# Attention and cosine FFN: conversions, splits and first gates tied to later products, mask added in PSUM

## The chip, the cores and the metric

The kernel runs on one core of one Trainium2 chip. The metric is the device time of one execution in microseconds (us); lower is better. Engines are named as in the profile: PE is TensorE (PEld its weight loads), DVE is VectorE, ACT is ScalarE, POOL is GpSimd, SP issues the DMA transfers.

## The reference

```python
scores = q @ k.T / sqrt(64)                       # 8 batches, 8 heads, 576 tokens, 64 per head
scores = where(mask[h], scores, -1e9)             # heads 0-3: the last 32 positions; heads 4-7: every 32nd position
attn = exp(scores - max) / (sum + 1e-9)
x = (attn @ v).transpose(0, 2, 1, 3).reshape(4608, 512)
h = x @ w_in                                      # 512 x 2048
out = (h * cos(h)) @ w_out                        # 2048 x 512
```

The weights arrive as 8-byte numbers (float64) and are turned into float32 on the chip. Every large product is made of fp32r values split into a high and a low part, as hi·hi + hi·lo + lo·hi.

## The kernel before

**Two phases.** Phase 1 (0 to about 521 us of the profiled execution) computes attention and h = x·w_in, and stores h to DRAM (`h_all`). Phase 2 (to 916 us) reads h back in 512-token pieces, computes g = h·cos(h) (`gate`), splits it, and multiplies by w_out (`outer`, line 583).

**Phase 1 by slots.** After a prologue that computes the attention of batch 0, a loop runs over slots, 56 per batch: 8 blocks `f` of 256 columns of h by `STEP` = 7 products. A product is 6 matmuls of 128x288 into a bank of PSUM (`m` three buffers, `n` and `o` one each). Batch 0 uses plain products (`FirstBlock`, line 470), the others a Winograd form with 7 products per block (`Block`, line 499): the products n0, n1 ... n6 stand at `SLOTS`, and after each `after0` ... `after6` copy a bank to SBUF on ACT (`kept`, line 507: m1, n1, m2) or finish a half of h (`hidden`: DVE line 517, ACT line 515). So n1's copy must end before the bank `n` is written by n4, three slots later, and the sum h<-m,n1 on DVE must end before n1's one SBUF tile is written by the next block.

**Other work between the slots.** Attention of the next batch comes as bursts of small matmuls some 8 slots apart (5 in batch 0), with a softmax on DVE, ACT and POOL (lines 236 to 256). In batches 0 and 1 the mask is written to PSUM by a matmul (line 226); from batch 2 on DVE adds it while it copies the scores to SBUF (line 244), takes the maximum (line 245), and POOL subtracts it (line 246). At the end of each batch the seven operands of the next (`x_hi`, `x_lo`) are formed (`Operands.sum` on DVE, line 431, and `make`, a split: ACT line 148, POOL line 149). In batch 0 each piece of w_in is loaded and converted (`to_float32`: two ACT steps, lines 133 and 139, two DVE steps, lines 140 and 143), split, and summed for the Winograd form (`weight_sums`); in batches 2 to 7 the same conversion goes over w_out, one piece per 17 slots, and the result is stored to DRAM (`w_all`), to be read and split in batch 7 (`output_weights`), in groups of three. The first three gates are issued in the last 14 slots of batch 7.

**Order.** A scheduler orders each engine's instructions by its own estimate of times. `order(later, first, ...)` adds a dependency without a semaphore that holds an instruction behind another in that schedule; `in_turn` chains all matmuls of the main loop, and `turn` is the last one. Only the first ACT step of a conversion is tied so (line 138).

Of the kernel before, what the change touches and what calls it, by code (L numbers as in the profile page):

```python
# [13 lines left out]
F32 = mybir.dt.float32  # L14
# [12 lines left out]
P = 128  # L27
# [36 lines left out]

UNITS = 7
# [13 lines left out]
def attention_cos_ffn(ctx, tc, qkl, vl, qkvs, w_in, w_out, eye, eye16, mask_l0, mask_l, mask_s, out):  # L79
# [45 lines left out]
    def to_float32(cv, src, out, bits=None):  # L125
        raw = cv.tile([P, 512, 2], I32, name="raw", bufs=3)
        load = nc.sync.dma_start(out=raw.rearrange("p n w -> p (n w)"), in_=src)
        if len(loads) == UNITS:
            order(load, loads[-1], "units first")
        low, top = raw[:, :, 0], raw[:, :, 1]  # L130
        scaled = top.bitcast(F32)
        bits = low if bits is None else bits
        begun = nc.scalar.activation(
            out=bits, in_=low.bitcast(U32), func=AF.Copy, scale=2.0 ** -29 * (1.0 - 2.0 ** -16),
            bias=7.5 * 2.0 ** -16 - 0.5,
        )
        if turn is not None:
            order(begun, turn, "with this product")
# [14 lines left out]
    def input_weights(cv, f, i):  # L153

        if i == 0:
            both = wp.tile([P, 6, 2 * P], I32, name="v")[:, :4]
            w = wp.tile([P, 2, 4, 2 * P], F32R, name="w")
            whole.append(both)
            wi.append(w)
        both, w = whole[f], wi[f]  # L160
        part = slice(2 * i, 2 * i + 2)
        name = "no"[i if f > 1 else 0]
        to_float32(
            cv, w_in.bitcast(I32)[2 * f + i], both[:, part].rearrange("p k n -> p (k n)"),
            pools[name].tile([P, 512], I32, name=name),
        )
        split(both[:, part].bitcast(F32), w[:, 0, part], w[:, 1, part])
        if i == 1:
            whole[f] = [both[:, n].bitcast(F32) for n in range(4)]
            wi[f] = [(w[:, 0, n], w[:, 1, n]) for n in range(4)]  # L170

    def weight_sums(cv, f, part):

        a11, a12, a21, a22 = whole[f][:4]
        if part == 0:
            sums = cv.tile([P, 3, 2 * P], F32, name="sums")
            whole[f].append(sums)
            s2, s3 = (sums[:, n] for n in range(2))
            first = nc.gpsimd.tensor_tensor(out=s3, in0=a11, in1=a21, op=ALU.subtract)
            order(first, turn, "with this product")  # L180
            nc.gpsimd.tensor_tensor(out=a21, in0=a21, in1=a22, op=ALU.add)
            split(a21, *wi[f][2])
            nc.gpsimd.tensor_tensor(out=s2, in0=a22, in1=s3, op=ALU.subtract)
        else:
            sums = whole[f][4]
            first = nc.gpsimd.tensor_tensor(out=sums[:, 2], in0=a12, in1=sums[:, 0], op=ALU.subtract)
            order(first, turn, "with this product")
            w = wp.tile([P, 2, 3, 2 * P], F32R, name="v")
            split(sums, w[:, 0], w[:, 1])
            wi[f] += [(w[:, 0, n], w[:, 1, n]) for n in range(3)]  # L190
# [5 lines left out]
    class Attention:  # L196
# [25 lines left out]
        def score_bank(self, b, mask):  # L222
            if b < 2:
                bank = self.bank(self.scores)
                n, w = mask.shape[1:]
                self.pe(nc.tensor.matmul(
                    bank[:, :n * w].rearrange("p (t w) -> p t w", w=w), ident16, mask, start=True, stop=False,
                    skip_group_check=True,
                ))
                return bank  # L230
            if self.kept is None:
                self.kept = self.bank(self.scores)
                nc.vector.memset(self.kept, 0.0)
            return self.kept

        def softmax(self, b, s, mask, n, w, pn=None):
# [33 lines left out]
        def local(self, b, u):  # L270
# [9 lines left out]
            def score(t, c):  # L280
                p, j = divmod(c, 2)
                self.scored = self.pe(nc.tensor.matmul(  # L282
                    s_ps[quarter_of(c), t * KW:(t + 1) * KW], q_t[half(j), p, QB * t:QB * (t + 1)],
                    k_t[half(j), p, QB * t:QB * t + KW], start=b > 1, stop=True, skip_group_check=True,
                ))
# [36 lines left out]
        def strided(self, b, p, u):  # L322
# [10 lines left out]
            def score(t, i):  # L333
                self.scored = self.pe(nc.tensor.matmul(  # L334
                    s_ps[half(1 - i, GB), t * GB:(t + 1) * GB], q_t[half(i), t], k_t[half(i), t],
                    start=b > 1, stop=True, skip_group_check=True,
                ))
# [73 lines left out]
    class Operands:  # L411
# [28 lines left out]
        def prepare(self, n):  # L440
            if n in (1, 3, 5, 6):
                self.sum(n)
            self.make(n)

# [38 lines left out]
    class Block:  # L483
# [21 lines left out]
        def kept(self, name):  # L505
            t = ev.tile([P, TH], F32, name=name)
# [38 lines left out]
    def whole_output_weights(cv, n):  # L545
        t = cv.tile([P, 3, 2 * P], F32, name="sums")[:, :2].rearrange("p k n -> p (k n)")
        to_float32(cv, w_out.bitcast(I32)[n], t.bitcast(I32))
        nc.sync.dma_start(out=w_all[n], in_=t)

    def output_weights(landed, g):  # L550
        w = wp.tile([P, 2, 4, 2 * P], F32R, name="w").rearrange("p f (l m) n -> p f l (m n)", l=2)
        v = wp.tile([P, 2, 3, 2 * P], F32R, name="v").rearrange("p l m n -> p (l m n)")
        parts = [v[:, :2 * DM].rearrange("p (l n) -> p l n", l=2), w[:, 0], w[:, 1]]
        for n in range(min(WG, NFC - WG * g)):
            both = landed.tile([P, DM], F32, name="both")
            nc.sync.dma_start(out=both, in_=w_all[WG * g + n])
            split(both, parts[n][:, 0], parts[n][:, 1])
            wo.append((parts[n][:, 0], parts[n][:, 1]))
# [3 lines left out]
    def gate(s, f):  # L562
# [34 lines left out]
    with ExitStack() as phase:  # L597
# [35 lines left out]
        for k, staged in enumerate(PROLOGUE):  # L633
# [4 lines left out]
            if k == 6:  # L638
                input_weights(cv, 0, 0)
                input_weights(cv, 0, 1)  # L640
                operands[0].split(0)
                operands[0].split(1)
        input_weights(cv, 1, 0)
        input_weights(cv, 1, 1)
# [21 lines left out]
        whole_at = {2 * PER_BATCH + 17 * n: n for n in range(NFC)}  # L666
        sums_at = {10 * f + 5 * part + 2 * STEP + 2: (f, part) for f in range(NF) for part in range(2)}
        for slot in range(max(plan) + 1):
# [7 lines left out]
            if b + 1 < B:  # L676
                if at == PER_BATCH - STEP - 1:
                    operands[b + 1] = Operands(b + 1)
                    for i in range(EXTRA):
                        operands[b + 1].prepare(i)  # L680
                if at - PER_BATCH + STEP in SLOTS[:7 - EXTRA]:
                    operands[b + 1].prepare(len(operands[b + 1].made))
            if b == 0 and at % STEP in (0, 4) and at // STEP + 2 < NF:
                input_weights(cv, at // STEP + 2, at % STEP // 4)
            if slot in whole_at:
                whole_output_weights(cv, whole_at[slot])
            if slot in sums_at:
                weight_sums(cv, *sums_at[slot])
            if b == B - 1:
# [7 lines left out]
                if at % STEP == 5 and at > STEP and len(wo) < NFC:  # L697
                    output_weights(more, len(wo) // WG)
# [7 lines left out]
    steps = [(s, f) for s in range(NTB) for f in range(NFC)]  # L706
    for i, (s, f) in enumerate(steps):
        if f == 0:
            acc = [ps_o.tile([P, DM], F32, name=f"acc{t}") for t in range(NTT)]
        if i + LAG < len(steps):  # L710
            pend.append(gate(*steps[i + LAG]))
# [96 lines left out]
```

## Time and profile before

| | |
|---|---|
| median of 3 runs | 920.88 us (919.09 to 921.38) |
| the profiled execution | 921.82 us, span 920.0 us, mean granted TensorE clock 0.989 |
| busy, share of the span | PE 97%, DVE 59%, ACT 58%, POOL 47% |
| phase 1, phase 2 | 0 to 520.8 us, 520.8 to 916 us |

A share says how much of the span an engine worked, not when: PE at 97% may wait for a few microseconds at places of which each has a cause of its own. "[idle before <-X]" in a row of the timeline is the time that the engine stood idle just before it and what ended it.

### The profile page before, as it was taken

The page shows a single profiled execution, that of the slowest core. Times are in us where ns is not written, and L with a number is a line of the kernel's source. Part 1 is how long each engine was busy: PE and PEld are TensorE (multiplying, and loading weights), DVE is VectorE, ACT ScalarE, POOL GpSimd, SP SyncE. Part 2 cuts the span into 40 slices and gives each one's busy share as a digit, 9 for nine tenths or more (in the row PEclk, how much of TensorE's full clock was granted, in tenths as well). Part 3 has the DMA queues.
Part 4 walks back from the last instruction along what each step waited for, and adds up shares of the span by engine and source line. Part 5 has one row for each costly group of instructions (what it writes and reads, how often), then busy time and mean ns, then how long its engine had stood idle before and what let it go on. Part 6 is the DMA issues. An engine that isn't in the chain of part 4 may idle for free.

```text
span 920.0 us, 21421 instructions
## 1 busy us (share of the span) xinstructions
PE 890.6 (97%) x8460; PEld 786.9 (86%) x8460; DVE 547.2 (59%) x918; ACT 529.1 (58%) x1020; POOL 428.9 (47%) x379
## 2 busy tenths in 40 slices
PE   9999889899999899999989999999999999999998
PEld 5788889899899799998989888888888888888886
DVE  5666645656556456665446266666666666666662
ACT  4656544444444245443457377777777777777773
POOL 2458986423425135243248344444444444444442
PEclk9899999999999999999999999999999999999999
DMA  9386444465655465554258334343434343434441
GB/s 340 122 276 224 143 139 149 171 212 187 203 181 191 159 212 199 189 187 148 100 176 263 131 94 146 92 140 102 138 102 139 94 148 92 141 100 138 116 126 46
DMA packets 70516, 143.83 MB, mean 156 GB/s; under 512 B 8208, under 2 KB 15632, under 8 KB 70416
## 3 DMA queue, kind: packets, MB, share of 16 engines
q1 hardware_dynamic: 69696, 142.24, 47.6%
q8 instruction: 66, 1.08, 0.5%
q14 instruction: 34, 0.28, 0.1%
q10 hardware_dynamic: 720, 0.23, 0.1%
HBM read 91.06 MB, written 51.38 MB: 155 GB/s over the span
## 4 chain that ended last, share of the span: by engine, by line
PE 72%; DMA 8%; POOL 6%; DVE 5%; issue 4%; ACT 3%; SPq 1%; ACTq 0%; POOLq 0%; DVEq 0%
PE acc L583 43%; PE m L499 14%; PE n L499 7%; DMA raw<-in_w_in 4%; PE o L499 3%; POOL x_lo L149 3%; DMA raw<-in_w_out 2%; PE acc L300 1%; PE acc L360 1%; PE acc L282 1%; DMA both<-w_all 1%; POOL v L149 1%; DVE v L143 1%; PE acc L334 1%; POOL e_sb L246 1%
## 5 line engine op out<-in xcount | busy, mean ns | idle before, releaser
L149 POOL TENSOR_TENSOR g_lo<-r,g_hi 128x512 fp32r<-128x512 f32 x144 | 187.5, 1302 | 214.6 <-ACT g_hi L148 200.7
L583 PE MATMUL acc<-w,g_hi 128*128 128x512 f32 x720 | 224.3, 393 | 0.0
L572 DVE TENSOR_TENSOR r<-r,h_in 128x512 f32<-128x512 f32 x144 | 154.6, 1074 | 101.5 <-ACT r L569 101.4
L583 PEld LDWEIGHTS acc<-w,g_hi 128*128 128x128 f32 x720 | 135.2, 188 | 29.3
L567 ACT ACTIVATE r<-h_in 128x512 int32<-128x512 f32 x144 | 91.1, 633 | 87.0 <-POOL g_lo L149 82.7
L583 PE MATMUL acc<-w,g_lo 128*128 128x512 f32 x360 | 139.7, 388 | 0.0
L583 PE MATMUL acc<-v,g_hi 128*128 128x512 f32 x432 | 134.6, 393 | 0.0
L568 DVE SCALAR_TENSOR_TENSOR r<-r,h_in 128x512 f32<-128x512 int32 x144 | 102.0, 708 | 29.9 <-ACT r L567 26.1
L569 ACT ACTIVATE r<-r,quarter 128x512 f32<-128x512 f32 x144 | 104.3, 725 | 19.3 <-DVE r L568 13.2
L499 PE MATMUL m<-x_hi,w 128*128 128x288 f32 x448 | 110.1, 300 | 2.9 <-DVE h L517 2.9
L499 PE MATMUL m<-x_hi,v 128*128 128x288 f32 x448 | 110.6, 302 | 2.1 <-ACT m L507 2.0
L583 PEld LDWEIGHTS acc<-v,g_hi 128*128 128x128 f32 x432 | 81.1, 188 | 17.5
L148 ACT CAST g_hi<-r 128x512 fp32r<-128x512 f32 x144 | 89.5, 622 | 7.1 <-PE acc L583 4.2
L246 POOL TENSOR_TENSOR e_sb<-e_sb,mx 128x324 f32<-128x324 f32 (+1 forms) x42 | 35.7, 849 | 104.2 <-DVE mx L245 87.9
L583 PE MATMUL acc<-v,g_lo 128*128 128x512 f32 x216 | 83.8, 388 | 0.0
L499 PEld LDWEIGHTS m<-x_hi,v 128*128 128x128 f32 x448 | 79.1, 190 | 4.4 <-ACT m L507 3.5
L499 PEld LDWEIGHTS m<-x_hi,w 128*128 128x128 f32 x448 | 78.2, 188 | 4.4 <-DVE h L517 3.4
L583 PEld LDWEIGHTS acc<-w,g_lo 128*128 128x128 f32 x360 | 67.6, 188 | 15.1
L507 ACT COPY m<-m 128x288 f32<-128x288 f32 x112 | 44.5, 397 | 42.5 <-PE m L499 40.7
L499 PE MATMUL m<-x_lo,v 128*128 128x288 f32 x224 | 66.7, 298 | 0.0
L499 PE MATMUL m<-x_lo,w 128*128 128x288 f32 x224 | 66.3, 296 | 0.0
L499 PE MATMUL n<-x_hi,v 128*128 128x288 f32 x224 | 55.6, 303 | 11.0 <-ACT n L507 11.0
(115 smaller groups left out, 1694.3 us busy)
## 6 DMA issues: line engine op xcount, KB each, us to landing
h_all<-h SPq DMA_DIRECT2D x128, 288.0 KB, 2.5
h_in<-h_all SPq DMA_DIRECT2D x144, 256.0 KB, 2.7
out<-o SPq DMA_DIRECT2D x36, 256.0 KB, 2.5
qk<-in_qkvs SPq DMA_DIRECT2D x28, 324.0 KB, 3.9
qk<-in_qkl SPq DMA_DIRECT2D x21, 416.0 KB, 4.1
raw<-in_w_in SPq DMA_DIRECT2D x16, 512.0 KB, 4.3
raw<-in_w_out SPq DMA_DIRECT2D x16, 512.0 KB, 4.1
v<-in_vl SPq DMA_DIRECT2D x24, 224.0 KB, 3.2
```

The costliest lines, as they stand in the source:

```text
L143: nc.vector.scalar_tensor_tensor(out=out, in0=top, scalar=3, in1=bits, op0=ALU.logical_shift_left, op1=ALU.bitwise_or)
L148: nc.scalar.copy(out=hi, in_=x)
L149: nc.gpsimd.tensor_tensor(out=lo, in0=x, in1=hi.bitcast(F32), op=ALU.subtract)
L246: nc.gpsimd.tensor_tensor(out=e, in0=e, in1=most, op=ALU.subtract)
L282: self.scored = self.pe(nc.tensor.matmul(s_ps[quarter_of(c), t * KW:(t + 1) * KW], q_t[half(j), p, QB * t:QB * (t + 1)], k_t[half(j), p, Q ...
L499: in_turn(nc.tensor.matmul(bank, a[:, c * P:(c + 1) * P], y[:, c], start=first and i == 0, stop=i == len(ops) - 1, skip_group_check=True,))
L507: nc.scalar.copy(out=t, in_=self.bank[name[0]])
L567: nc.scalar.activation(out=k, in_=h, func=AF.Copy, scale=1.0 / (2.0 * math.pi), bias=0.25)
L568: nc.vector.scalar_tensor_tensor(out=r, in0=k, scalar=-2.0 * math.pi, in1=h, op0=ALU.mult, op1=ALU.add)
L569: sin = nc.scalar.activation(out=r, in_=r, func=AF.Sin, bias=quarter)
L572: nc.vector.tensor_tensor(out=r, in0=r, in1=h, op=ALU.mult)
L583: in_turn(nc.tensor.matmul(acc[t], g[:, at], w, start=(f == 0 and i == 0), stop=(f == NFC - 1 and i == 2)))
```

## The change

- A conversion is in steps: the load (`land`) is issued 8 slots (w_in) or 10 slots (w_out) ahead, both ACT steps are tied to one product, the split follows two slots later. The read of a converted piece of w_out stands 6 slots ahead of its split, and pieces come one by one instead of by three. The sums of the weights are in four steps. Tiles `w` are half as large and twice as many.
- The operands' sums and splits are tied to the slots of `PREPARED` (47 to 57 of the batch before).
- `score_bank` uses the cleared bank without mask matmul from batch 1 on; the mask is added in place in PSUM, the maximum is taken and subtracted from PSUM, all on DVE.
- n1 has two SBUF tiles.
- The first step and the Sin of each of the first gates are tied to the product at whose slot they are issued.

```diff
+PREPARED = ((None, 47), (47, 48), (None, 50), (50, 53), (None, 54), (53, 55), (54, 57))
...
+    def with_product(begun):
+        if turn is not None:
+            order(begun, turn, "with this product")
+
+    def land(cv, src):
         raw = cv.tile([P, 512, 2], I32, name="raw", bufs=3)
         load = nc.sync.dma_start(out=raw.rearrange("p n w -> p (n w)"), in_=src)
...
-        begun = nc.scalar.activation(
+        with_product(nc.scalar.activation(
...
-        nc.scalar.activation(out=scaled, in_=scaled, func=AF.Copy, scale=2.0 ** -112)
+        with_product(nc.scalar.activation(out=scaled, in_=scaled, func=AF.Copy, scale=2.0 ** -112))
...
     def split(x, hi, lo):
-        nc.scalar.copy(out=hi, in_=x)
+        with_product(nc.scalar.copy(out=hi, in_=x))
         nc.gpsimd.tensor_tensor(out=lo, in0=x, in1=hi.bitcast(F32), op=ALU.subtract)
...
         def score_bank(self, b, mask):
-            if b < 2:
+            if b == 0:
...
-            if b < 2:
+            if b == 0:
                 nc.vector.tensor_reduce(out=mx[:, :n], in_=s, op=ALU.max, axis=AX.X)
                 nc.vector.tensor_tensor(out=e, in0=s, in1=most, op=ALU.subtract)
             else:
-                nc.vector.tensor_tensor(out=e, in0=s, in1=mask, op=ALU.add)
-                nc.vector.tensor_reduce(out=mx[:, :n], in_=e, op=ALU.max, axis=AX.X)
-                nc.gpsimd.tensor_tensor(out=e, in0=e, in1=most, op=ALU.subtract)
+                nc.vector.tensor_tensor(out=s, in0=s, in1=mask, op=ALU.add)
+                nc.vector.tensor_reduce(out=mx[:, :n], in_=s, op=ALU.max, axis=AX.X)
+                nc.vector.tensor_tensor(out=e, in0=s, in1=most, op=ALU.subtract)
...
         def kept(self, name):
-            t = ev.tile([P, TH], F32, name=name)
+            t = ev.tile([P, TH], F32, name=name, bufs=2 if name == "n1" else 1)
...
-        nc.scalar.activation(out=k, in_=h, func=AF.Copy, scale=1.0 / (2.0 * math.pi), bias=0.25)
+        with_product(nc.scalar.activation(out=k, in_=h, func=AF.Copy, scale=1.0 / (2.0 * math.pi), bias=0.25))
...
         sin = nc.scalar.activation(out=r, in_=r, func=AF.Sin, bias=quarter)
+        with_product(sin)
...
+        for n in range(2, NF):
+            for i in range(2):
+                at = 7 * n + 7 * i // 2 - 13
+                in_steps(input_weights(cv, n, i), max(at - 8, 0), at, at + 2)
+        for f in range(NF):
+            in_steps(weight_sums(cv, f), *(16 + 10 * f + i for i in (0, 2, 5, 7)))
+        for n in range(NFC):
+            at = 2 * PER_BATCH + 17 * n
+            in_steps(whole_output_weights(cv, n), at - 10, at)
+        for n in range(NFC):
+            at = (B - 1) * PER_BATCH + STEP * (n // WG) + 12 + 2 * (n % WG)
+            in_steps(output_weights(n), at - 6, at)
+        for b in range(1, B):
+            for i, (summed, made) in enumerate(PREPARED):
...
+                if summed:
+                    steps.setdefault(at + summed, []).append(partial(lambda b, i: operands[b].sum(i), b, i))
+                steps.setdefault(at + made, []).append(partial(lambda b, i: operands[b].make(i), b, i))
```

What this does to an engine's order is shown at three places. The first is ACT in the first two blocks of batch 4, before: `raw` is a loaded piece of w_out, L133 and L139 the two ACT steps of a conversion, `n` and `m` with a number are the copies n1 and m1 or m2 (L507), L515 is a half of h.

```order
L247 ACTIVATE e_sb<-e_sb 128x324
L133 ACTIVATE raw<-raw 128x512
L507 COPY m_4695<-m 128x288
L515 COPY h<-m 128x288
L507 COPY m_4720<-m 128x288
L368 COPY x_4644<-acc_4738 128x6x18x3
L374 COPY x_4644<-acc_4738 128x18x2
L139 ACTIVATE raw<-raw 128x512
L507 COPY n_4792<-n 128x288
```

And there after the change:

```order
L250 ACTIVATE e_sb<-e_sb 128x324
L505 COPY n_4690<-n 128x288
L142 ACTIVATE raw<-raw 128x512
L146 ACTIVATE raw<-raw 128x512
L505 COPY m_4698<-m 128x288
L513 COPY h<-m 128x288
L505 COPY m_4723<-m 128x288
L371 COPY x_4643<-acc_4739 128x4x18x3
```

Before, the second step (L139) that stands between the copies belongs to the next piece, whose load is the latest in the queue; after, both steps (L142, L146) stand together, behind n1's copy, and belong to one piece.

The second place is POOL at the end of batch 3, where the operands of batch 4 are split (`x_lo`); `pn_s` and e_sb<-e_sb,z are products with 1/sum of the softmax, e_sb<-e_sb,mx the subtraction of the maximum. Before:

```order
L149 TENSOR_TENSOR x_lo<-t,x_hi 128x576
L253 TENSOR_TENSOR pn_s_115<-e_sb,z 128x6x54
L246 TENSOR_TENSOR e_sb<-e_sb,mx 128x324
L253 TENSOR_TENSOR pn_s_116<-e_sb,z 128x6x54
L246 TENSOR_TENSOR e_sb<-e_sb,mx 128x384
L149 TENSOR_TENSOR x_lo<-x_3968,x_hi 128x576
L149 TENSOR_TENSOR x_lo<-t,x_hi 128x576
L149 TENSOR_TENSOR x_lo<-x_3968,x_hi 128x576
L253 TENSOR_TENSOR e_sb<-e_sb,z 128x384
L149 TENSOR_TENSOR x_lo<-t,x_hi 128x576 x2
```

And after:

```order
L256 TENSOR_TENSOR pn_s_115<-e_sb,z 128x6x54
L256 TENSOR_TENSOR pn_s_116<-e_sb,z 128x6x54
L156 TENSOR_TENSOR x_lo<-x_3711,x_hi 128x576
L156 TENSOR_TENSOR x_lo<-t,x_hi 128x576
L156 TENSOR_TENSOR x_lo<-x_3969,x_hi 128x576
L256 TENSOR_TENSOR e_sb<-e_sb,z 128x384
L156 TENSOR_TENSOR x_lo<-t,x_hi 128x576
L156 TENSOR_TENSOR x_lo<-x_3969,x_hi 128x576
L156 TENSOR_TENSOR x_lo<-t,x_hi 128x576 x2
```

The first two splits stood ahead of the two pn_s (the second of them is the first row before); now all seven stand in one row behind them with one product between, and the subtractions of the maximum are gone from POOL.

The third place is ACT in batch 7. Before, at its first two blocks (L567 is the first step of a gate, L569 its Sin, which needs another table, `both` a piece of w_out that was read back):

```order
L567 ACTIVATE r<-h_in 128x512
L507 COPY m_7379<-m 128x288
L567 ACTIVATE r<-h_in 128x512
L148 CAST v<-both 128x512
L569 ACT_TABLE_LOAD
L569 ACTIVATE r<-r,quarter 128x512 x2
L507 COPY n_7405<-n 128x288
```

After, the first gate's steps (L571, L573) are here, in the sixth and seventh block:

```order
L155 CAST w<-both 128x512
L571 ACTIVATE r<-h_in 128x512
L505 COPY m_7749<-m 128x288
L573 ACT_TABLE_LOAD
L573 ACTIVATE r<-r,quarter 128x512
L155 CAST v<-both 128x512
L505 COPY n_7790<-n 128x288
L155 CAST g_hi<-r 128x512
L571 ACTIVATE r<-h_in 128x512
```

The order of the scheduler had drawn the first gates to the start of the batch; now they stand where the loop issues them. PE's order differs only in the seven mask matmuls of batch 1, and the order of phase 2 is the same.

## Rows read from the trace of the kernel before

**Rows 1.** Busy time by stage: batch 0, batches 1 to 7, phase 2.

```profile
core 0: us, PE busy (x) PEld busy (x) DVE busy (x) ACT busy (x) POOL busy (x), PEclk, DMA share, GB/s
25.00:110.00 85.00, 77.97 (x1143) 71.61 (x1141) 52.82 (x117) 48.57 (x109) 56.58 (x58) 0.92 0.60 201
110.00:310.00 200.00, 189.05 (x2677) 180.64 (x2676) 113.30 (x245) 88.98 (x218) 96.58 (x97) 0.99 0.52 175
310.00:470.00 160.00, 158.05 (x2228) 152.16 (x2228) 90.00 (x192) 70.57 (x173) 57.37 (x53) 0.99 0.49 165
470.00:520.80 50.80, 46.02 (x333) 44.38 (x332) 22.26 (x36) 29.79 (x64) 29.37 (x22) 1.00 0.71 234
520.80:916.00 395.20, 395.20 (x1728) 324.16 (x1727) 254.10 (x293) 279.37 (x435) 181.87 (x140) 1.00 0.38 112
```

**Rows 2.** What PE waited for: us in total, times, longest us.

```profile
PE n L499 <- ACT n L507: 11.0, 6, 3.4
PE m L470 <- ACT h L479: 4.5, 2, 2.8
PE m L499 <- DVE h L517: 2.9, 2, 2.4
PE n L499 <- DVE h L517: 1.6, 3, 0.9
PE acc L226 <- DVE e_sb L242: 1.2, 1, 1.2
```

**Rows 3.** What ACT waited for, as Rows 2.

```profile
ACT raw L139 <- DMA raw<-in_w_out: 31.4, 16, 5.3
ACT raw L139 <- DMA raw<-in_w_in: 19.2, 10, 3.2
```

**Rows 4.** Timeline of ACT from 299 us.

```profile
307.31 0.65 ACT L139 ACTIVATE raw<-raw 128x512 f32<-128x512 f32 x1 [5.31 <-DMA raw<-in_w_out]
```

**Rows 5.** Busy time by stretch, as Rows 1; first and last of four.

```profile
70.80:74.20 3.40, 3.40 (x64) 2.86 (x67) 1.94 (x5) 1.60 (x3) 3.40 (x5) 0.50 0.56 185
...
309.80:313.00 3.20, 3.20 (x15) 3.12 (x13) 0.59 (x2) 0.40 (x1) 0.68 (x1) 0.50 0.49 184
```

**Rows 6.** DMA issues: KB each, median us from issue to landing.

```profile
raw<-in_w_in SPq DMA_DIRECT2D x16, 512.0 KB, 4.3
```

**Rows 7.** Instructions by shape, DVE: busy, mean ns, idle before.

```profile
L431 DVE TENSOR_TENSOR t<-x,x 128x576 f32<-128x576 f32 x7 | 5.3, 764 | 0.3
L242 DVE TENSOR_TENSOR e_sb<-acc,mx 128x324 f32<-128x324 f32 x4 | 1.9, 486 | 0.0
```

**Rows 8.** Instructions by shape, POOL: busy, mean ns, idle before.

```profile
L149 POOL TENSOR_TENSOR x_lo<-t,x_hi 128x576 fp32r<-128x576 f32 x28 | 43.0, 1548 | 0.9 <-ACT x_hi L148 0.9
L246 POOL TENSOR_TENSOR e_sb<-e_sb,mx 128x324 f32<-128x324 f32 x24 | 19.2, 802 | 24.8 <-DVE mx L245 24.8
```

**Rows 9.** Timeline of DVE from 173 us.

```profile
174.07 1.96 DVE L431 TENSOR_TENSOR t<-x,t 128x576 f32<-128x576 f32 x1 [0.81 <-POOL x_lo L149]
175.95 0.45 DVE L517 TENSOR_TENSOR h<-n,m 128x288 f32<-128x288 f32 x1
```

**Rows 10.** Timeline of POOL there.

```profile
175.37 3.33 POOL L149 TENSOR_TENSOR x_lo<-t,x_hi 128x576 fp32r<-128x576 f32 x2
```

**Rows 11.** Instructions of line 226, PE, from 25 to 90 us, by shape.

```profile
L226 PE MATMUL acc<-ms,ident 128*128 128x324 bf16 x4 | 1.2, 312 | 1.2 <-DVE e_sb L242 1.2
L226 PE MATMUL acc<-ml,ident 128*128 128x384 bf16 x3 | 1.2, 405 | 0.0
```

**Rows 12.** Timeline of ACT from 476 us.

```profile
476.46 0.63 ACT L567 ACTIVATE r<-h_in 128x512 int32<-128x512 f32 x1 [3.44 <-DMA h_in<-h_all]
478.44 1.28 ACT L569 ACT_TABLE_LOAD   x1
480.97 0.38 ACT L507 COPY n<-n 128x288 f32<-128x288 f32 x1
```

More of the change, by code (lines that the diff above doesn't have):

```diff
@@ L129, in to_float32 @@
             order(load, loads[-1], "units first")
+        return raw
+    def to_float32(raw, out, bits=None):
         low, top = raw[:, :, 0], raw[:, :, 1]
@@ L153, in input_weights @@
     def input_weights(cv, f, i):
+        raw = land(cv, w_in.bitcast(I32)[2 * f + i])
+        yield
         if i == 0:
[L156 to L160, printed above, removed]
+            whole.append(wp.tile([P, 6, 2 * P], I32, name="v")[:, :4])
+            wi.append([])
         part = slice(2 * i, 2 * i + 2)
         name = "no"[i if f > 1 else 0]
[L163 to L190, printed above, removed]
+        both = whole[f][:, part]
@@ new lines, in input_weights, with weight_sums @@
+        to_float32(raw, both.rearrange("p k n -> p (k n)"), pools[name].tile([P, 512], I32, name=name))
+        yield
+        w = wp.tile([P, 2, 2, 2 * P], F32R, name="w", bufs=2 * NF)
+        split(both.bitcast(F32), w[:, 0], w[:, 1])
+        wi[f] += [(w[:, 0, n], w[:, 1, n]) for n in range(2)]
+        yield
+    def weight_sums(cv, f):
+        a11, a12, a21, a22 = (whole[f][:, n].bitcast(F32) for n in range(4))
+        sums = cv.tile([P, 3, 2 * P], F32, name="sums")
+        s2, s3, s4 = (sums[:, n] for n in range(3))
+        with_product(nc.gpsimd.tensor_tensor(out=s3, in0=a11, in1=a21, op=ALU.subtract))
+        nc.gpsimd.tensor_tensor(out=a21, in0=a21, in1=a22, op=ALU.add)
+        yield
+        split(a21, *wi[f][2])
+        nc.gpsimd.tensor_tensor(out=s2, in0=a22, in1=s3, op=ALU.subtract)
+        yield
+        with_product(nc.gpsimd.tensor_tensor(out=s4, in0=a12, in1=s2, op=ALU.subtract))
+        yield
+        w = wp.tile([P, 2, 3, 2 * P], F32R, name="v")
+        split(sums, w[:, 0], w[:, 1])
+        wi[f] += [(w[:, 0, n], w[:, 1, n]) for n in range(3)]
+        yield
@@ L438, in make @@
             self.made.append((hi, lo))
[L440 to L443, printed above, removed]
     class FirstOperands:
@@ L545, in whole_output_weights, with output_weights @@
     def whole_output_weights(cv, n):
+        raw = land(cv, w_out.bitcast(I32)[n])
+        yield
         t = cv.tile([P, 3, 2 * P], F32, name="sums")[:, :2].rearrange("p k n -> p (k n)")
-        to_float32(cv, w_out.bitcast(I32)[n], t.bitcast(I32))
+        to_float32(raw, t.bitcast(I32))
         nc.sync.dma_start(out=w_all[n], in_=t)
[L550 to L558, printed above, removed]
+        yield
+    def output_weights(n):
+        if n % WG:
+            t = wp.tile([P, 2, 2, 2 * P], F32R, name="w", bufs=2 * NF).rearrange("p l m n -> p l (m n)")
+        else:
+            t = wp.tile([P, 2, 3, 2 * P], F32R, name="v").rearrange("p l m n -> p (l m n)")
+            t = t[:, :2 * DM].rearrange("p (l n) -> p l n", l=2)
+        both = more.tile([P, DM], F32, name="both")
+        nc.sync.dma_start(out=both, in_=w_all[n])
+        yield
+        split(both, t[:, 0], t[:, 1])
+        wo.append((t[:, 0], t[:, 1]))
+        yield
     wo, pend = [], []
@@ L665, in attention_cos_ffn, with in_steps @@
                 plan[STEP * i + slot] = partial(block.product, n)
-        whole_at = {2 * PER_BATCH + 17 * n: n for n in range(NFC)}
-        sums_at = {10 * f + 5 * part + 2 * STEP + 2: (f, part) for f in range(NF) for part in range(2)}
+        steps = {}
+        def in_steps(work, *slots):
+            work = iter(work)
+            for slot in slots:
+                steps.setdefault(slot, []).append(partial(next, work, None))
+        for n in range(2, NF):
+            for i in range(2):
+                at = 7 * n + 7 * i // 2 - 13
[10 more added lines that the diff above has]
+            for i, (summed, made) in enumerate(PREPARED):
+                at = (b - 1) * PER_BATCH
+                if i == 0:
+                    steps.setdefault(at + made, []).append(partial(lambda b: operands.update({b: Operands(b)}), b))
+                if summed:
+                    steps.setdefault(at + summed, []).append(partial(lambda b, i: operands[b].sum(i), b, i))
+                steps.setdefault(at + made, []).append(partial(lambda b, i: operands[b].make(i), b, i))
         for slot in range(max(plan) + 1):
@@ L675, in attention_cos_ffn @@
                 next(unit)
[L676 to L688, printed above, removed]
+            for step in steps.get(slot, ()):
+                step()
             if b == B - 1:
@@ L705, in attention_cos_ffn @@
     ps_o = ctx.enter_context(tc.tile_pool(name="ps_o", bufs=2, space=bass.MemoryType.PSUM, reuse_waits="tile"))
-    steps = [(s, f) for s in range(NTB) for f in range(NFC)]
-    for i, (s, f) in enumerate(steps):
+    tiles = [(s, f) for s in range(NTB) for f in range(NFC)]
+    for i, (s, f) in enumerate(tiles):
         if f == 0:
             acc = [ps_o.tile([P, DM], F32, name=f"acc{t}") for t in range(NTT)]
-        if i + LAG < len(steps):
-            pend.append(gate(*steps[i + LAG]))
+        if i + LAG < len(tiles):
+            pend.append(gate(*tiles[i + LAG]))
         outer(s, f, *pend.pop(0), acc)
```

18 lines of the change are left out of this document (6 added, 12 removed).

## The prediction

> **What bounds the kernel now.** I read the busy times by stage first, because PE works 97% of the span and only its gaps, its clock and its own instructions can be won [rows 1]. Phase 2 is 395.20 us of which PE is busy 395.20, at full clock: nothing to win there, and the change leaves its order alone. The gaps are in phase 1: 85 − 77.97 = 7.0 us in batch 0 (25 to 110 us), 200 − 189.05 = 10.9 us from 110 to 310, 2.0 us from 310 to 470, and 50.8 − 46.02 = 4.8 us in the last batch; 24.7 us in all.
>
> The waits of PE say who ends the gaps [rows 2]: ACT's copies of n (11.0 us in 6 waits), ACT's copies of h in batch 0 (4.5 in 2), DVE's sums of h. Such a copy takes 0.38 us [rows 12]; so the question is why they come late, and that is read on their own engines. ACT waits for landing loads of weights more than for most things: 31.4 us for w_out, 19.2 us for w_in, always at L139 [rows 3]. The timeline shows what that costs: at 302 us ACT reaches the L139 of a piece that is still on its way, stands 5.31 us, and behind it stands n1's copy [rows 4]. The longest wait of PE for n, 3.4 us, is this one [rows 2]. The piece that it waits for is one that nothing needs yet: the second ACT step is not tied to a product, and the scheduler put it ahead of copies that are needed at once.
>
> A gap has an aftermath. The granted clock is 0.50 (1.2 instead of 2.4 GHz) in four stretches of about 3.4 us, of which two are shown [rows 5]; the others are 94.8 to 98 and 122.1 to 125.3. PE had stood idle a few microseconds ahead of each: the stretch from 309.8 follows the gap that ended with ACT's wait of [rows 4]. Half speed for 3.4 us loses 1.7 us, 6.8 us for four. Three of them follow gaps made by loads, one (122) the start of batch 1.
>
> **The change, part by part.**
>
> *Conversions tied, loads 8 to 10 slots ahead.* A load takes 4.3 us in the median [rows 6]; the 410.8 us from 110 to 520.8 hold 7 batches of 56 slots, so a slot is 1.05 us and 8 of them 8.4 us. Both ACT steps now stand together behind a product that comes after the load has landed. That removes the 4.5 us of waits for h and the 1.2 us of a score bank that DVE released late in batch 0 (DVE's first step waited for ACT's), and the 3.4 us in batch 4: 9.1 us; with three slow stretches of 1.7 us, 14.2. The ACT steps themselves (0.65 us each [rows 4]) stay; they are covered by the two to three slots that a copy has, and if they were not, each pair of 1.3 us would be seen as a wait for n. I take nine tenths, 12.8 us, because three buffers of raw still bound how far ahead loads run in batch 0, where transfers are already busy 0.60 of the time [rows 1]. Nothing won is the lower end (fourth rival), 14.2 the upper.
>
> *First gates and w_out in batch 7.* Before, ACT waits 3.44 us for the first h_in, loads a table (1.28 us) and does Sin ahead of n1's copy, which comes at 480.97 [rows 12]. The change moves this to the sixth and seventh block, a point at which there is no attention left and h_in has long landed, and spreads the reads of w_out. The last batch's 4.8 us become, as I take it, 1.2 (the table load still stands ahead of one m1 or n1 copy, and three gates' POOL steps are later than they were): 3.6 us won, of 0 to 4.8. What is late next would be the fourth gate; its chain from the last product is one step each of ACT, ACT, DVE, ACT and POOL, against three gates in stock that cover 3 × 2.75 us of PE (395.20 us over 144 pieces).
>
> *Softmax in PSUM.* POOL loses 42 subtractions of about 0.8 us [rows 8], and the hand-over from DVE to POOL and on to ACT. DVE gains 42 subtractions from PSUM, for which the rows of batch 1 have a price, 0.49 us for 324 columns [rows 7]; and seven mask additions: 25 us, spread over 400. DVE is busy 113 of 200 us there [rows 1], so the work has room on average; the scores' bank is held about 1.0 us longer, against 8 slots until the next scores write it. Writing PSUM in place is not in the trace; if it took twice the addition into SBUF (0.5 us more), that would still be covered where DVE has room. I cost it at nothing on the path, but see the second rival. PE loses seven mask matmuls in batch 0's slots [rows 11]. Their rows say 2.4 us busy, in which the modelled ends overlap what follows; I take 0.25 of the 0.31 to 0.41 of each, 1.7 us, between 0 (if bursts waited for scores' bank anyway) and 2.4.
>
> *n1 in two tiles, operands at their slots.* The other gaps from 110 to 470 us, 10.9 − 3.4 + 2.0 = 9.5 us, and the slow stretch at 122 (1.7 us), lie almost all at the ends of batches, where operands are formed: POOL holds 7 x_lo of 1.55 us [rows 8] in the row, DVE four subtractions, ACT seven casts, beside the copies. There the sums of h come late: h<-m,n1 on DVE is behind a t that took 1.96 us and a conversion of 1.90 [rows 9] while POOL did two x_lo [rows 10], and PE waited 2.4 us for it [rows 2]. The change takes POOL's and DVE's conversions out of the first boundary, n1's copy no longer waits for that sum, and POOL has one subtraction fewer there per burst. Against that, the seven x_lo are now all in the last 10 slots; 7 × 1.55 = 10.8 us, in a stretch of 10 slots, 10.5 us. Followed row by row with these durations, at one boundary (batch 3 to 4), h<-m,n1 and n1's copies end 0.2 to 1 us before PE needs them, and t for the last operand waits for an x_lo. So some are late: I take 0.7 us per boundary for six boundaries, 4.2 us, that stay: 11.2 − 4.2 = 7.0 won, between a loss (third rival) and 11.2.
>
> *Small gaps* of batch 0 (7.0 − 5.7 = 1.3 us, x and pt on ACT): 0.5 us won.
>
> On the resource that the crowded boundary shares, the trace shows this: t, which reads two tiles in SBUF, took 1.96 us beside POOL's x_lo [rows 9, 10], against 0.76 us when nothing stood beside it [rows 7], while h<-n,m, which reads one bank of PSUM and one SBUF tile, kept its 0.45 us beside the second x_lo. The Trainium skill ("SBUF — State Buffer", section Who interferes with whom) says just this: an instruction of VectorE with two SBUF inputs contends with GpSimd's reads for a shared port pair, taken as an exclusive lock, and one with at most one SBUF input doesn't. The trace agrees. By that rule moving the subtraction of the maximum into PSUM costs DVE nothing at POOL's hands, but the four t beside seven x_lo stay exposed and each pair stretches; that is the mechanism of the third rival.
>
> **Sum.** 12.8 + 3.6 + 1.7 + 7.0 + 0.5 = 25.6 us. The profiled execution took 921.82: 896.2. It lies 0.9 us above the median of the runs, 920.88, so 895.3 against that.
>
> **The rivals.**
> 1. *All of it goes.* Every gap, the four slow stretches and the mask matmuls: 24.7 + 6.8 + 1.7 = 33.2 us, 888. For it: nearly three batches, from 310 to 470 us, have only 2.0 us of gaps already [rows 1]. Against: the crowded boundary.
> 2. *DVE and POOL late at the boundary, moderately.* Each of the seven boundaries has one wait like the 2.4 us for h [rows 2], and three of them a slow stretch: 7 × 2.4 + 3 × 1.7 = 21.9 instead of 4.2 us, 17.7 more: 914. For it: DVE has a subtraction more in each burst, and in the order of after a subtraction from PSUM stands ahead of h<-m,n1. Against: h<-m,n1 has four slots to spare.
> 3. *Slower: operands tied too late.* Before, x_lo 0 and 1 were done ahead of the softmax's pn_s; now they are behind. If the first split starts 3 us late and the seven take 1.66 us each (3.33 for two [rows 10]), the last product of the old batch and the third of the new one wait 3.3 us and each boundary also loses a slow stretch: 7 × 5.0 = 35 us where there were 11.2, against 18.6 won elsewhere: 921.8 + 35 − 11.2 − 18.6 = 927. It decides from (11.2 + 18.6) / 7 = 4.3 us per boundary. Against: POOL has 0.8 us less in each burst, and the loop could be followed without such a wait.
> 4. *The change doesn't do what it says.* Loads still are what the conversions wait for, in batch 0 through the three raw buffers and later through transfers of h that stand in the same queue: the 12.8 us stay, 908.
>
> **How the numbers follow.** Forecast 0.60 (its own range 890 to 902), first rival 0.10, second 0.14, third 0.06, fourth 0.06, and 0.04 for a mixture that comes out near no change. The range of 888 to 913 leaves out the third rival, the mixture, half of the second and a little of the first, about 2 in 10. About 0.3% (2.8 us) is what a measurement of this kernel can tell from no change. Faster: 0.60 + 0.10 + 0.14 + 0.06 = 0.90; slower 0.07 (third, and a part of the mixture), same 0.03.
>
> **What would show it.** In the profile after: no wait of ACT's conversion steps for landing loads; PE's waits in batch 0 and in batch 4 gone, and the granted clock 1.00 in stages after batch 0; n1's copy at the start of batch 7 not behind a table load; phase 2 unchanged at 395.2 us; POOL some 35 us less, DVE some 25 us more. Wrong would be: PE waiting at every end of batch for a sum of h or an x_lo for over 2 us (second and third rival), conversions waiting on loads (fourth), or a wait of PE for the first gates at 520 us less what was won.

## The result and the profile after

The changed kernel takes 891.16 us in the median (890.38 to 891.71, 4 runs) against 921.13 for the one before on the same chip: a ratio of 0.967, 95% interval 0.964 to 0.970, so 30 us less, between 28 and 33. The forecast of 895.3 was 4 us too high, and the range held it. Its size was nearly right; where it came from was only in part, as the experiments show. Three executions far slower than the rest (the profiled ones of e4 and e5, 1843 and 4847 us, and one of the kernel before beside e9 to e12, 1424 us) are left out of the medians below, so e4 and e5 have no profile that can be read.

The busy times of the changed kernel by stage, with the stages of [rows 1] at its own times (batch 0, batches 1 to 7, phase 2):

```profile
core 0: us, PE busy (x) PEld busy (x) DVE busy (x) ACT busy (x) POOL busy (x), PEclk, DMA share, GB/s
25.00:104.00 79.00, 78.50 (x1218) 73.70 (x1217) 61.73 (x132) 49.62 (x110) 58.72 (x57) 0.96 0.69 226
104.00:290.00 186.00, 183.76 (x2662) 176.47 (x2664) 121.22 (x264) 87.70 (x215) 77.54 (x72) 1.00 0.56 188
290.00:439.00 149.00, 148.84 (x2131) 143.63 (x2132) 94.84 (x204) 69.08 (x168) 39.86 (x33) 1.00 0.51 172
439.00:488.60 49.60, 48.91 (x364) 48.32 (x363) 20.02 (x34) 30.46 (x65) 30.73 (x24) 1.00 0.65 217
488.60:884.00 395.40, 395.40 (x1730) 324.38 (x1730) 257.30 (x299) 282.42 (x440) 183.33 (x142) 1.00 0.40 115
```

PE's idle time between prologue and phase 2 was 24.7 us and is 0.5 + 2.2 + 0.2 + 0.7 = 3.6, so 21.1 us went. The granted clock is 1.00 from 104 us on (the 0.96 of batch 0 is one slow stretch at its start, which the kernel before has too), so four stretches that lost 1.7 us each went, 6.8 us. Seven mask matmuls are 1.7 by the prediction's estimate. That is 29.6 of the 31.4 us by which the span is shorter (920.0 to 888.6); e5 and e12 come back to the rest. Phase 2 is as it was. What PE still waits for, with the columns of [rows 2]:

```profile
PE m L497 <- DVE h L515: 1.6, 2, 1.1
PE n L497 <- ACT n L505: 0.9, 2, 0.6
PE n L497 <- DVE h L515: 0.3, 1, 0.3
```

Of ACT's waits for a landing piece of w_in or w_out, 50.6 us in [rows 3], 0.4 us is left. POOL's work went from 428.9 to 396.9 us, DVE's from 547.2 to 569.6.

### The profile page after: what moved, and what is told of

Same layout as the page of the kernel before. It is cut to its first block, busy times and chain, and to the rows that moved or that the text cites. A ratio compares the mean times of both kernels' runs of the same rounds, so it can differ in the third digit from the quotient of the medians.

```text
span 888.6 us, 21381 instructions
## 1 busy us (share of the span) xinstructions
PE 880.3 (99%) x8453; PEld 780.9 (88%) x8453; DVE 569.6 (64%) x967; ACT 531.0 (60%) x1020; POOL 396.9 (45%) x337
## 4 chain that ended last, share of the span: by engine, by line
PE 89%; POOL 3%; DVE 2%; DMA 2%; ACT 2%; issue 2%; SPq 0%; ACTq 0%; POOLq 0%
PE acc L588 45%; PE m L497 18%; PE n L497 9%; PE m L468 5%; PE o L497 4%; PE acc L303 2%; PE acc L285 2%; PE acc L363 2%; POOL x_lo L156 1%; PE acc L337 1%; DMA raw<-in_w_in 1%; PE acc L350 1%; DMA both<-w_all 1%; DMA v<-in_qkvs 0%; POOL v L156 0%
## 5 line engine op out<-in xcount | busy, mean ns | idle before, releaser
L571 ACT ACTIVATE r<-h_in 128x512 int32<-128x512 f32 x144 | 91.2, 633 | 80.5 <-POOL g_lo L156 80.3
L573 ACT ACTIVATE r<-r,quarter 128x512 f32<-128x512 f32 x144 | 104.3, 724 | 20.6 <-DVE r L572 15.9
L256 POOL TENSOR_TENSOR pn_s<-e_sb,z 128x324 f32<-128x324 f32 x32 | 23.3, 729 | 102.5 <-DVE z L254 77.8
L256 POOL TENSOR_TENSOR e_sb<-e_sb,z 128x384 f32<-128x384 f32 x24 | 20.4, 851 | 85.8 <-DVE z L254 76.2
```

The costliest lines, as they stand in the source:

```text
L256: nc.gpsimd.tensor_tensor(out=pn, in0=e, in1=z[:, :n].unsqueeze(2).broadcast_to([P, n, w]), op=ALU.mult)
L571: with_product(nc.scalar.activation(out=k, in_=h, func=AF.Copy, scale=1.0 / (2.0 * math.pi), bias=0.25))
```

## The experiments

Each is a part undone in the changed kernel ("after less ..."), or a part alone on the kernel before. Times are medians; ratios are to the kernel before on the same chip, whose median was 920.5 us beside e1 to e4, 923.2 beside e5 to e8 and 922.8 beside e9 to e12, so differences between runs are given by medians and by ratios where the two part.

**e1: before, with the second ACT step tied.**

```diff
-        nc.scalar.activation(out=scaled, in_=scaled, func=AF.Copy, scale=2.0 ** -112)
+        begun = nc.scalar.activation(out=scaled, in_=scaled, func=AF.Copy, scale=2.0 ** -112)
+        if turn is not None:
+            order(begun, turn, "with this product")
```

> The kernel before with one thing of the change: the second ACT step of a conversion is tied to the same product as the first. Theory (the untied second step, which is scheduled ahead of urgent copies and waits for a load that nothing needs yet, is what made the waits of batch 0 and batch 4): 10 us of gaps and up to three slow stretches of 1.7 us go, so 905 to 909 us, and no wait of ACT for raw over 1 us after batch 0. Rival (the loads must be issued 8 to 10 slots ahead for this): 918 to 922 us, ACT still waits for raw.

Measured: 907.59 us, ratio 0.986 (0.984 to 0.988). The theory. In its profile PE's waits in batch 0 ahead of 102 us are gone; the stages read like this:

```profile
25.00:102.00 77.00, 76.50 (x1162) 71.67 (x1160) 52.37 (x117) 47.96 (x106) 57.82 (x58) 0.96 0.69 223
102.00:300.00 198.00, 190.34 (x2714) 181.98 (x2716) 113.45 (x246) 89.21 (x218) 96.80 (x97) 0.98 0.54 179
300.00:457.00 157.00, 154.96 (x2195) 149.65 (x2186) 90.63 (x192) 71.96 (x176) 58.49 (x53) 1.00 0.50 168
457.00:507.00 50.00, 46.13 (x324) 44.50 (x323) 20.43 (x35) 30.00 (x64) 27.67 (x21) 0.97 0.72 231
```

Batch 0 is without gaps, and 7.7, 2.0 and 3.9 us of idle time remain in the other stages: ends of batches and first gates. So 10.6 of the 24.7 us of gaps went. The three slow stretches behind gaps made by loads went too, but with the one at the start of batch 1 (now from 111.7 us) there are two others, from 173.1 and 466.7 us (clock 0.50 for 3.4 us each), behind gaps that the loads hadn't made.

**e2: after, less the tie of the second ACT step.**

```diff
-        with_product(nc.scalar.activation(out=scaled, in_=scaled, func=AF.Copy, scale=2.0 ** -112))
+        nc.scalar.activation(out=scaled, in_=scaled, func=AF.Copy, scale=2.0 ** -112)
```

> The changed kernel with the second ACT step of a conversion untied again; everything else of the change stays. Theory (the tie does it): ACT waits some 50 us for raw again and PE has gaps behind late copies of n, m or h of 6 to 12 us with slow stretches behind the longest: 899 to 908 us. Rival (the early loads do it, with or without the tie): 891 to 893 us.

Measured: 907.18 us, ratio 0.986 (0.983 to 0.989), 16 us above the changed kernel. The theory, at the upper end. ACT's waits are back nearly to the number of [rows 3]:

```profile
ACT raw L146 <- DMA raw<-in_w_out: 32.4, 15, 5.8
ACT raw L146 <- DMA raw<-in_w_in: 17.5, 9, 3.2
```

This is what one of them does, in ACT's timeline of e2:

```profile
279.37 0.66 ACT L146 ACTIVATE raw<-raw 128x512 f32<-128x512 f32 x1 [5.85 <-DMA raw<-in_w_out]
279.93 0.30 ACT L322 COPY x<-acc 128x192 f32<-128x192 f32 x1
280.13 0.68 ACT L155 CAST x_hi<-t 128x576 fp32r<-128x576 f32 x1
280.70 0.40 ACT L505 COPY m<-m 128x288 f32<-128x288 f32 x1
```

And in PE's:

```profile
281.15 0.40 PE L497 MATMUL m<-x_hi,v 128*128 128x288 f32 x1 [1.80 <-ACT m L505]
...
285.15 0.61 PE L497 MATMUL m<-x_hi,w 128*128 128x288 f32 x1 [2.93 <-DVE h L515]
```

The copy of m stands third behind the step that waited 5.85 us. Here the wait fell on the end of a batch, where operands' casts queue up behind it as well, and PE stopped twice; the granted clock was 0.50 from 282.6 to 289.2 us.

**e3: after, with the loads written where they are converted.**

```diff
-                in_steps(input_weights(cv, n, i), max(at - 8, 0), at, at + 2)
+                in_steps(input_weights(cv, n, i), at, at, at + 2)
...
-            in_steps(whole_output_weights(cv, n), at - 10, at)
+            in_steps(whole_output_weights(cv, n), at, at)
```

> The changed kernel with the load of each piece of weights written at the slot of its conversion instead of 8 or 10 slots ahead; the ties stay. Theory (the tie does it, and the scheduler issues a load as soon as a buffer is free, wherever it is written): 890 to 893 us, no wait for raw. Rival (the lead does it): each of 28 conversions waits up to 4 us on ACT and the copies behind it come late, 900 to 915 us.

Measured: 890.20 us, ratio 0.967 (0.964 to 0.969). The theory: the lead of 8 or 10 slots does nothing, because it doesn't reach the chip. The order of instructions on SP, ACT, DVE and POOL is the same in both kernels; a load is bound to no product and is issued once one of three buffers is free. So this run is a second measurement of the changed kernel's order, and what a load that really starts earlier or later is worth was not measured.

**e4: after, with the old softmax and mask matmuls in batch 1.** Edit: the two conditions `b == 0` of `score_bank` and `softmax` back to `b < 2`, `start=b > 0` of the scores' matmuls back to `b > 1`, and the three lines of `softmax` as before.

> The changed kernel with the softmax of before: mask matmuls in batch 1, mask added from PSUM to SBUF, the maximum subtracted by POOL. Theory (the softmax in PSUM matters only through seven mask matmuls; the ends of batches run because conversions and operands stand at fixed slots): 892.5 to 894 us. Rival (taking 36 us off POOL is what clears the ends of batches): waits of PE for n and h of 1 to 3 us at most ends of batches, 898 to 904 us.

Measured: 901.78 us, ratio 0.980 (0.978 to 0.982), 11 us above the changed kernel (12 by ratios). The theory fell: the softmax is worth 11 us, not 1.7. e5, e6 and e12 take it apart.

**e5 and e12: after, with POOL subtracting the maximum, and no mask matmul.**

```diff
-                nc.vector.tensor_tensor(out=s, in0=s, in1=mask, op=ALU.add)
-                nc.vector.tensor_reduce(out=mx[:, :n], in_=s, op=ALU.max, axis=AX.X)
-                nc.vector.tensor_tensor(out=e, in0=s, in1=most, op=ALU.subtract)
+                nc.vector.tensor_tensor(out=e, in0=s, in1=mask, op=ALU.add)
+                nc.vector.tensor_reduce(out=mx[:, :n], in_=e, op=ALU.max, axis=AX.X)
+                nc.gpsimd.tensor_tensor(out=e, in0=e, in1=most, op=ALU.subtract)
```

> The changed kernel with POOL subtracting the maximum again (mask added from PSUM to SBUF by DVE, as before from batch 2 on; no mask matmuls; PE's order the same). Rival that the old softmax brought up (POOL's subtractions, 36 us in a queue with the splits, make exp and the copies behind it late): 899 to 902 us, with waits of PE for n and h behind ACT's exp that waits for POOL. Theory as it was (the softmax matters only through the mask matmuls): 891 to 893 us.

> The kernel of the run with POOL's subtraction once more, for its profile: 897 to 900 us, 7 to 8 us of gaps more than after the change, at ends of batches, where POOL's splits stand ahead of a subtraction that exp on ACT, and the copies behind exp, wait for.

Measured: 897.97 us, ratio 0.973 (0.968 to 0.977), and again 897.21, 0.973 (0.970 to 0.977): the rival, a little below its range. That is 6 to 7 us above the changed kernel by medians and 5 by ratios for the subtraction, so some 4 to 7 of e4's 11 go with the mask matmuls of batch 1. In e1, which has these seven and no wait of PE at any of them, the next matmul starts 0.24 to 0.27 us after each, 1.75 us in all: what the prediction took. What the other 2 to 5 us are isn't shown, as e4 has no profile to read. The mechanism of the subtraction is in the timelines of e12 at the start of batch 5, POOL, ACT and PE in turn:

```profile
337.64 1.88 POOL L156 TENSOR_TENSOR x_lo<-t,x_hi 128x576 fp32r<-128x576 f32 x1
339.47 1.18 POOL L249 TENSOR_TENSOR e_sb<-e_sb,mx 128x324 f32<-128x324 f32 x1
...
340.69 0.47 ACT L250 ACTIVATE e_sb<-e_sb 128x324 f32<-128x324 f32 x1 [2.66 <-POOL e_sb L249]
341.06 0.38 ACT L505 COPY n<-n 128x288 f32<-128x288 f32 x1
...
341.50 0.40 PE L497 MATMUL n<-x_hi,v 128*128 128x288 f32 x1 [1.55 <-ACT n L505]
341.74 0.29 PE L497 MATMUL n<-x_lo,v 128*128 128x288 f32 x1
341.87 0.30 PE L497 MATMUL n<-x_hi,v 128*128 128x288 f32 x1
```

The subtraction waits behind the last x_lo; exp on ACT waits 2.66 us for it; n1's copy is behind exp; PE waits 1.55 us for the copy. (The last two rows start 0.13 us apart though each is about 0.29 long: a gap is counted from the modelled end of a matmul, and so, by an estimate from these rows, costs about 0.16 us more than its row says. PE's waits, without that of the warm-up, went from 21 to 6; fifteen times 0.16 is about 2 us, near the 1.8 that the account of the result left over.)

**e6: after, with maximum and subtraction in SBUF, still on DVE.**

```diff
-                nc.vector.tensor_tensor(out=s, in0=s, in1=mask, op=ALU.add)
-                nc.vector.tensor_reduce(out=mx[:, :n], in_=s, op=ALU.max, axis=AX.X)
-                nc.vector.tensor_tensor(out=e, in0=s, in1=most, op=ALU.subtract)
+                nc.vector.tensor_tensor(out=e, in0=s, in1=mask, op=ALU.add)
+                nc.vector.tensor_reduce(out=mx[:, :n], in_=e, op=ALU.max, axis=AX.X)
+                nc.vector.tensor_tensor(out=e, in0=e, in1=most, op=ALU.subtract)
```

> The changed kernel with the mask added from PSUM to SBUF and maximum and subtraction made in SBUF, all three on DVE as after the change; the order of the other engines is the same. If it is POOL's relief that counts, 890 to 893 us; if it counts that DVE works in PSUM and not in SBUF beside POOL, the subtraction and additions are longer beside POOL's splits and the time is 895 us or more.

Measured: 898.86 us, ratio 0.974 (0.970 to 0.978). POOL is relieved just as after the change, every engine has the same instructions in the same order, and 7.7 us are lost (6 by ratios). So it counts that the subtraction reads PSUM: for 324 columns the addition takes 0.49 us in e6 and 0.50 after the change, the maximum 0.49 in both, and only the subtraction differs. Line 249 of e6 and then of the changed kernel (count: ns least/median/most):

```profile
L249 DVE TENSOR_TENSOR e_sb<-e_sb,mx x49: 480/557/1907, 39.0 to 420.5; 128x324 f32<-128x324 f32 x28, 128x384 f32<-128x384 f32 x21
```

```profile
L249 DVE TENSOR_TENSOR e_sb<-acc,mx x49: 476/495/558, 40.5 to 414.2; 128x324 f32<-128x324 f32 x28, 128x384 f32<-128x384 f32 x21
```

Alone it takes as long in SBUF as in PSUM; beside POOL up to four times as long: each of the 18 executions in e6 that took over 0.6 us (0.61 to 1.91) started while an instruction of POOL was under way, and the other 31 took at most 0.56. The timelines of e6 at the start of batch 6, POOL, DVE, ACT:

```profile
394.58 3.33 POOL L156 TENSOR_TENSOR x_lo<-t,x_hi 128x576 fp32r<-128x576 f32 x2
...
396.92 1.35 DVE L249 TENSOR_TENSOR e_sb<-e_sb,mx 128x324 f32<-128x324 f32 x1
...
398.30 0.47 ACT L250 ACTIVATE e_sb<-e_sb 128x324 f32<-128x324 f32 x1 [1.66 <-DVE e_sb L249]
398.68 0.38 ACT L505 COPY n<-n 128x288 f32<-128x288 f32 x1
```

The same place in the changed kernel:

```profile
389.09 3.35 POOL L156 TENSOR_TENSOR x_lo<-t,x_hi 128x576 fp32r<-128x576 f32 x2
...
391.44 0.48 DVE L249 TENSOR_TENSOR e_sb<-acc,mx 128x324 f32<-128x324 f32 x1
...
391.96 0.47 ACT L250 ACTIVATE e_sb<-e_sb 128x324 f32<-128x324 f32 x1 [0.81 <-DVE e_sb L249]
392.34 0.38 ACT L505 COPY n<-n 128x288 f32<-128x288 f32 x1
```

In e6 the subtraction runs on until after the x_lo ends at 397.9 us; in the changed kernel it takes 0.48 us beside the same pair of x_lo. The Trainium skill ("SBUF — State Buffer", section Who interferes with whom) has the rule that the prediction cited, that an instruction of VectorE with two SBUF inputs contends with GpSimd's reads and one with a single SBUF input doesn't; the runs agree, with 1.35 against 0.48 us.

**e7: before, with the second ACT step tied and the new softmax** (the edits of e1 and of the change's softmax).

> The kernel before with the second ACT step tied and the new softmax; operands, weight sums, splits, first gates and n1 as before. If the two parts simply add up: 907.6 less 11, 895 to 898 us, and the rest (some 5 us) is first gates and fixed slots. If the softmax only helps where operands stand at fixed slots: 903 to 906 us.

Measured: 895.76 us, ratio 0.970 (0.967 to 0.974), 12 us less than e1. The parts add up. Of e1's 9.7 us of gaps between batch 0 and the last batch 4.6 are left, and neither of its two slow stretches there. The last batch still has its gaps: PE is busy 47.01 of 51.00 us from 442 to 493.

**e8: after, with one tile for n1** (`bufs=2 if name == "n1" else 1` taken out).

> The changed kernel with one SBUF tile for n1. Theory (the second tile takes away a wait that matters at some ends of batches only): 891 to 894 us, ACT waits for DVE's h at n1's copy some 5 us in total. Rival (it is what clears the ends of batches): 897 us or more, PE waiting over 1 us for n at most of them.

Measured: 890.74 us, ratio 0.965 (0.961 to 0.968): the second tile is worth nothing. ACT waits 1.8 us for h at n1's copy, not the 5 expected.

**e9: after, with the first gates not tied** (both `with_product` in `gate` taken out).

> The changed kernel with the first gates' first step and Sin not tied. Theory: ACT meets the table load and Sin ahead of n1's copy at the start of the last batch again, gaps of 0.9 and 2 us and perhaps a slow stretch: 894 to 897 us, all of it in the last batch. Rival (what the last batch won came from w_out piece by piece): 890 to 892 us.

Measured: 897.19 us, ratio 0.972 (0.968 to 0.975). The theory, at its upper end. ACT's timeline is that of [rows 12] again, at the start of the last batch:

```profile
451.32 0.63 ACT L571 ACTIVATE r<-h_in 128x512 int32<-128x512 f32 x1 [3.48 <-DMA h_in<-h_all]
451.86 0.38 ACT L505 COPY m<-m 128x288 f32<-128x288 f32 x1
452.28 0.63 ACT L571 ACTIVATE r<-h_in 128x512 int32<-128x512 f32 x1
452.94 1.28 ACT L573 ACT_TABLE_LOAD   x1
...
455.99 0.38 ACT L505 COPY n<-n 128x288 f32<-128x288 f32 x1
```

n1's copy stands behind the table load and Sin, and PE waited 2.3 us for it; its waits in the last batch are 5.8 us, against 0.6 in the changed kernel. The loss is 6 us by medians and 4 by ratios; the four runs spread from 893.4 to 899.0. From e7 to e11 the same part brings 4.4, or 3.5 by ratios.

**e10: after, with the operands at the slots of before and their casts not tied.** Edit: the calls of `prepare` at the end of each batch as before instead of `PREPARED`, and `split` without `with_product` there.

> The changed kernel with sums and splits of the operands written at the slots of before and their ACT casts not tied, so that the scheduler draws the first two ahead again. Theory after the earlier runs (conversions, softmax and gates hold nearly all of it; the fixed slots are worth nothing): 889 to 893 us. Rival (the fixed slots keep the ends of batches clear): 894 us or more, with waits for n and h over 1 us at several ends of batches.

Measured: 895.54 us, ratio 0.971 (0.969 to 0.973), 4.4 us above the changed kernel (3.7 by ratios). The rival, but not as it put it: the loss is nearly all at the first end of a batch. POOL and then ACT there:

```profile
105.72 2.80 POOL L158 TENSOR_TENSOR x_lo<-t,x_hi 128x576 fp32r<-128x576 f32 x2
108.48 0.83 POOL L258 TENSOR_TENSOR e_sb<-e_sb,z 128x384 f32<-128x384 f32 x1
109.27 0.72 POOL L184 TENSOR_TENSOR sums<-v 128x256 f32<-128x256 f32 x1
110.08 0.72 POOL L185 TENSOR_TENSOR v<-v 128x256 f32<-128x256 f32 x1
...
110.83 0.41 ACT L155 CAST w<-v 128x256 fp32r<-128x256 f32 x1 [2.65 <-POOL v L185]
111.14 0.39 ACT L512 COPY n<-n 128x288 f32<-128x288 f32 x1
```

A sum of weights stands behind x_lo on POOL, a cast tied to its product waits 2.65 us for it, and n1's copy stands behind the cast: the pattern of the loads with POOL in the load's place. PE waited 2.3 us, and the granted clock was 0.50 from 111.3 to 114.7 us.

**e11: before, with three parts of the change: second ACT step tied, softmax in PSUM, first gates tied** (e7 and the two `order` calls in `gate`).

> The kernel before with three parts of the change alone: second ACT step tied, softmax in PSUM, first gates tied; loads, splits, weight sums, operands, w_out by threes and n1 as before. Theory (these three are all): 889.5 to 892 us. Rival (the other parts add): 893 us or more.

Measured: 891.38 us, ratio 0.967 (0.965 to 0.969): the changed kernel's ratio. Its profile keeps 1.8 us of wait for n at the first end of a batch and 2.5 for h at three others, and a slow stretch of 3.4 us follows the first. The changed kernel has 0.9 and 1.9 us of such waits and no stretch there, so all that e11 leaves out is worth no more than about 3 us, too little to be told apart between the two intervals.

## Why the prediction was right, and where it was not

**Right: what the loads did.** The wait of L139 for a load that nothing needs was read as the cause of the gaps in batches 0 and 4 and the slow stretches behind them, priced at 12.8 of 14.2 us; e1 gives 13 us and e2 takes 16. The sum is right and its parts less so: 9.1 us of gaps and three slow stretches were priced, and e1 shows 10.6 us of gaps and one stretch fewer, since two came elsewhere. The nine tenths were too careful, and the reason for them (three buffers bound the lead) was beside the point: with the tie alone (e1) the waits go, without it (e2) they are back, and the lead changes no engine's order (e3). So the fourth rival had no ground.

**Right: the first gates,** 3.6 us predicted; 3.5 to 4.4 from e7 to e11, and 4 to 6 in e9.

**Wrong in its size: the softmax.** "I cost it at nothing on the path" beside 1.7 us for the mask matmuls was the step that failed. On top of e1 it brought 12 us, undone it costs 11: 5 to 7 for the subtraction, 1.75 for the mask matmuls as predicted, and a rest of 2 to 5 us that goes with them and is open. Average room on DVE and POOL was the wrong measure: exp waits for the subtraction, the copies stand behind exp on ACT, and at the end of a batch POOL has two x_lo in front of its subtraction. The prediction had the rows for it (the 1.96 us of t beside x_lo, [rows 9]) and used the rule on the shared ports to say that the subtraction costs DVE nothing in PSUM, and for the third rival, but not for what the subtraction's place is worth.

**Wrong in its ground: the ends of batches.** 7.0 us were credited to two tiles of n1, the operands' slots, and conversions out of the way. n1 is worth nothing (e8), the slots something, nearly all of it at the first end of a batch (e10, and within about 3 us in e11). Most of what was won there is the softmax's: from e1 to e7 5.1 us of gaps and two slow stretches went. This error and the one above offset each other in the sum: that the total came out so near was in part luck. The 0.7 us that should stay at each end of a batch were in fact 0 to 1.1, above 0.3 at two of them.

**The rivals.** Nearly all of it went, 30 of 33.2: the time lies between the forecast and the first rival, a little nearer the rival. The second (DVE late by one more subtraction) did not come: in PSUM it takes 0.48 us for 324 columns, near the 0.49 of [rows 7], and the addition in place 0.50; the longest subtraction, of 384 columns, took 0.56. The third (operands too late) is refuted: the fixed slots help or do nothing. The fourth is refuted by the 0.4 us of waits for loads that are left.

**What stays open.** What makes up the 2 to 5 us between e4 and e5 beyond the seven matmuls' own time. Undone one at a time, the tie, the softmax, the gates and the operands cost 16 + 11 + 6 + 4 = 37 us by medians, more than the 30 that they brought together: so some gaps would need more than one of them to close, which is argued and was not followed gap by gap.

## What to carry to other kernels

Where a scheduler may move instructions, look on each in-order engine for one that waits for something that nobody needs yet and stands ahead of copies that PE needs at once; one dependency that holds it back here was worth 13 us, while writing its load 8 to 10 slots earlier changed no engine's order. When elementwise work is moved, ask first what stands behind it on the next engine and beside it on the same ports: the same instruction on the same engine in the same order cost 6 to 8 us more with both operands in SBUF than with one of them in PSUM. A sum that comes out right can have two wrong terms; undo parts one by one, and put the few that matter alone on the old kernel.

## What the runs showed that was not expected

A slow stretch at the start of batch 0 comes and goes between executions that do the same: e3 has the changed kernel's order on its engines, and e9 the same prologue. From 25 to 45 us the granted clock was, in the changed kernel, in e3 and in e9:

```profile
25.00:45.00 20.00, 19.50 (x290) 17.03 (x289) 14.98 (x37) 12.20 (x30) 10.69 (x10) 0.83 0.46 143
```

```profile
25.00:45.00 20.00, 19.33 (x310) 17.27 (x308) 16.51 (x40) 13.95 (x34) 11.05 (x11) 1.00 0.58 187
```

```profile
25.00:45.00 20.00, 19.32 (x279) 16.89 (x278) 13.92 (x35) 12.30 (x30) 10.12 (x10) 0.74 0.44 130
```

At 0.83, 1.00 and 0.74 of 20 us, with PE busy 19.3 to 19.5 us in each, that is 3.4, 0 and 5.2 us lost. Runs of one kernel differ by 1 to 7 us here, and such stretches would explain part of it: e3's four ran at a mean clock of 1.000, 0.996, 0.996 and 0.996, the first in 887.56 and the others in 889.8 to 890.6 us. A comparison of two single profiles has to take it out. Without what was lost from 25 to 45 us (0 in e7, 1.8 in e6 and e12, 3.4 in e1 and e11, 5.2 in e10), the profiled executions lie above the changed kernel's by 1 us in e3, 2 in e11, 5 in e10, 7 in e9 and e12, 8 in e7 and in e6, and e7 10 us below e1: the account above stands, with e11's 2 us for all the parts that it leaves out.
